# A Fourier and mixer kernel: a chunk's second product goes into the other PSUM bank, and the block sums move away from the GpSimd adds

## The chip, the cores and the metric

The kernel runs on one core of a Trainium2 chip. The metric is the device time of one execution, in microseconds. Three runs of the kernel before are given, and one more execution was taken with the hardware profiler; its trace is what the profile shows.

## What is computed

The input x has 8 batches of 3008 tokens with 256 features. The reference takes a Fourier transform along tokens and features and keeps the real part, and then applies a mixer block: two matrix products along the tokens and two along the features, each with a relu between and a residual added.

```python
X = np.fft.fft(x, axis=1)
X = np.fft.fft(X, axis=2)
x = X.real
xt = x.transpose(0, 2, 1)
h = np.maximum(xt @ w_tok1, 0.0) @ w_tok2
u = x + h.transpose(0, 2, 1)
h2 = np.maximum(u @ w_ch1, 0.0) @ w_ch2
return u + h2
```

The shapes are w_tok1 (3008, 256), w_tok2 (256, 3008), w_ch1 (256, 1536) and w_ch2 (1536, 256).

## The kernel before

**The stages of a batch.** `fold` (VectorE, called DVE here; lines 414 to 433) adds mirrored features of x into `eo`. `front` (lines 436 to 567) does the transform and the token mixing as a sequence of small pieces, each ended by a `yield`: pieces with pz (line 445), pieces with pw and w (lines 472 to 477), `tok1` (pt, line 488, and uv), `third` (pq and py, then ACT's qs, then two DVE adds into yt, lines 514 to 527), and the pieces that make `ut`, the transposed u of one chunk (pu, line 552, and a DVE add, line 560). The PSUM tiles of these pieces rotate through three buffers (`ps_f`).

**The chunks.** A batch has 6 chunks of 512 tokens. For each chunk `mm1` (lines 584 to 597) multiplies by w_ch1 in 12 tiles of 128 hidden features and ACT writes the relu into c1. `mm2` multiplies c1 by w_ch2. Most chunks do that in `mm2_sums` (line 620), which saves one block product in eight: c1 is seen as 2 by 2 blocks (token halves by hidden halves), w_ch2 as 2 by 2 blocks (hidden halves by feature halves), and 7 products of 12 matmuls of 128x128 each give the four output blocks. They need sums of blocks: those of the weights are made once (`weight_sums`), those of c1 are made per chunk on DVE by `block_sums` (lines 599 to 609). Its four entries are called sum 0 to sum 3 here. Sums 0, 1 and 3 go into the tile sb, sum 2 overwrites a block of c1. Each sum is made in two halves of three tiles: k from 0 to 2 while the chunk is still in `mm1`, k from 3 to 5 one chunk later. First chunk of batch 0, the last chunk of even batches and the last chunk of all are plain (line 579) and use no sums.

**The order of the work.** All orders are written out by hand; each engine runs its own queue in the order of the calls and waits on semaphores. The main loop (lines 772 to 817) has four steps s for each chunk c. A step calls `mm1` for three tiles, takes some pieces of `own` (the rest of this batch's front) and of `nxt` (the next batch's front), and calls step s of `mm2` for the chunk before; `plan` and `own_plan` say how many pieces stand in which of a batch's 24 steps. DVE's folds are taken from the eleventh step of a batch on in batches 1 to 5.

**The seven products.** The tiles px and py are two PSUM banks, each seen as two halves: pa is px, pb is py. Products are accumulated in pa[:,0] over the four steps, and ACT copies the intermediate states to the tile m (`keep`, line 638). The steps of `mm2_sums` are:

- step 0: a product into pa[:,0] and one into pa[:,1], keep(0), a DVE add of pa[:,1] and m into the output tile osb, and a GpSimd add of the residual rt (128x256)
- step 1: a product of sb[:,0] into pb[:,0], a product of sb[:,1] on top of pa[:,0], keep(1)
- step 2: a product on top of pa[:,0], keep(2), a DVE add from pb[:,0]
- step 3: a product on pa[:,0], a product with sb[:,2] on pb[:,0], two DVE adds (first from px, then from py), a GpSimd add of the residual (128x512), and the stores

The DVE and GpSimd adds go through `residual` (line 618). `edges` (line 611) copies one or two columns inside rt, which a transposing DMA has filled one chunk earlier (`turn_u`, line 571). GpSimd's queue also issues the loads of x (lines 128 and 118).

Of the kernel before, what the change touches and what calls it, by code (L numbers as in the profile page):

```python
# [40 lines left out]
def kernel(  # L41
# [9 lines left out]
    nc = tc.nc  # L51
# [17 lines left out]
    def ps_out(name):  # L69
        return psum.tile([P, 512], FP32, tag="o2", name=name, bufs=2)  # L70
# [4 lines left out]
    def dram(t, offset, ap):  # L75
        return bass.AP(tensor=t, offset=offset, ap=ap)
# [84 lines left out]
    for t in (tp, tq):  # L161
        for i in range(2):
            h = slice(64 * i, 64 * i + 64)
            nc.scalar.activation(
                out=t[h, :, 64 - 64 * i:128 - 64 * i],
                in_=pcol[h, :].unsqueeze(2).to_broadcast([64, NG, 64]),
                func=AFT.Copy, scale=0.0)
    nc.scalar.activation(out=w1m[64:128, NG - 1, :],
                         in_=pcol[64:128, :].to_broadcast([64, DTOK]),
# [43 lines left out]
    wc2 = const.tile([P, NCT, D], FP16, tag="wc2")  # L213
# [8 lines left out]
    HC = NCT // 2  # L222
    wst = const.tile([P, 4, HC, P], FP16, tag="wst")
# [8 lines left out]
    def swap_wc1(h):  # L232
        nc.sync.dma_start(out=wc1[1][:, h, :], in_=wc1[0][:, h, :])
        nc.sync.dma_start(out=wc1[1][0:1, h, :], in_=wc1[0][0:1, 1 - h, :])
# [172 lines left out]
    def align_w2(j):  # L407
        th, k = j // 4, slice(16 * (j % 4), 16 * (j % 4) + 16)
        copy(0, w2p[:, th, k, 0:NQ], w2v[:, th, k, :])
# [171 lines left out]
    def plain(b, c):  # L581
        return (b, c) == (0, 0) or c + 1 == NCH and (b % 2 == 0 or b + 1 == BB)
# [16 lines left out]
    def block_sums(c1, sb, k, which):  # L599
        hi = slice(HC + k.start, HC + k.stop)  # L600
        a11, a21 = c1[:, k, 0:D], c1[:, k, D:CW]
        a12, a22 = c1[:, hi, 0:D], c1[:, hi, D:CW]
        sums = ((sb[:, 0, k], a21, a22, AT.add),
                (sb[:, 1, k], sb[:, 0, k], a11, AT.subtract),
                (a21, a11, a21, AT.subtract),
                (sb[:, 2, k], a12, sb[:, 1, k], AT.subtract))
        for i in which:
            o, x, y, op = sums[i]
            nc.vector.tensor_tensor(out=o, in0=x, in1=y, op=op)  # L609

    def edges(rt, c):
        for o, i in ((D, 0), (0, P)) if c >= 3 else ((D, P),):
            nc.vector.tensor_copy(out=rt[:, :, o:o + 1], in_=rt[:, :, i:i + 1])

    lower, upper, turned_ = slice(0, P), slice(P, D), slice(D, P, -1)

    def residual(eng, o, x, y):
        eng.tensor_tensor(out=o, in0=x, in1=y, op=AT.add)  # L618

    def mm2_sums(b, c, c1, s, box):  # L620
        if s == 0:
            box["osb"] = work.tile([P, 4, D], FP32, tag="osb", name="osb", bufs=3)
            box["m"] = work.tile([P, 3, 2, P], FP32, tag="m", name="m")
            box["po"] = ps_out("px"), ps_out("py")
            edges(box["rt"], c)
        osb, rt, sb, m = (box[i] for i in ("osb", "rt", "sb", "m"))
        pa, pb = (p[:].rearrange("p (i t d) -> p i t d", i=2, t=2) for p in box["po"])

        def product(o, a, hi, w, first=False):
            for t in range(2):  # L630
                f = D * hi + P * t
                for k in range(HC):
                    nc.tensor.matmul(o[:, t], lhsT=a(k)[:, f:f + P], rhs=w(k),  # L633
                                     start=(first and t == 0 and k == 0),
                                     stop=(k == HC - 1), skip_group_check=True)

        def keep(i):
            nc.scalar.activation(out=m[:, i], in_=pa[:, 0], func=AFT.Copy)  # L638

        v, g = nc.vector, nc.gpsimd  # L640
        if s == 0:
            product(pa[:, 0], lambda k: c1[:, k], 0, lambda k: wc2[:, k, lower], True)
            product(pa[:, 1], lambda k: c1[:, HC + k], 0, lambda k: wc2[:, HC + k, lower])
            keep(0)
            residual(v, osb[:, 0:2, lower], pa[:, 1], m[:, 0])
            residual(g, osb[:, 0:2, lower], osb[:, 0:2, lower], rt[:, 0:2, lower])
        elif s == 1:
            product(pb[:, 0], lambda k: sb[:, 0, k], 0, lambda k: wst[:, 0, k], True)
            product(pa[:, 0], lambda k: sb[:, 1, k], 0, lambda k: wst[:, 1, k])
            keep(1)  # L650
        elif s == 2:
            product(pa[:, 0], lambda k: c1[:, k], 1, lambda k: wst[:, 2, k])
            keep(2)
            residual(v, osb[:, 2:4, upper], pb[:, 0], m[:, 2])
        else:
            product(pa[:, 0], lambda k: c1[:, HC + k], 1, lambda k: wst[:, 3, k])
            product(pb[:, 0], lambda k: sb[:, 2, k], 0, lambda k: wc2[:, HC + k, upper])
            residual(v, osb[:, 2:4, lower], pa[:, 0], rt[:, 2:4, lower])
            residual(v, osb[:, 0:2, upper], pb[:, 0], m[:, 1])
            residual(g, osb[:, :, upper], osb[:, :, upper], rt[:, :, turned_])  # L660
        if s == 3:
            for i in range(2):
                nk = 3 if c + 1 == NCH and i else 4
                nc.sync.dma_start(
                    out=dram(out_t, (b * S + 8 * c + i) * D,
                             [[NQ * D, 64], [2 * D, nk], [1, D]]),
                    in_=osb[64 * i:64 * i + 64, 0:nk, :])
            if c + 1 == NCH:
                nc.sync.dma_start(
                    out=dram(out_t, ((b - 1) * S + NQ - 1) * D, [[NQ * D, 64], [1, D]]),  # L670
                    in_=osb[64:P, 3, :])
# [45 lines left out]
    def pair(b, c1):  # L717

        if b % 2 == 0 and b + 1 < BB:
            state["ch"] = work.tile([P, NCT, 64], FP16, tag="ch", name="ch")  # L720
            nc.vector.tensor_copy(out=state["ch"][:], in_=c1[:, :, CW - 128:CW - 64])
        elif b % 2:
            nc.vector.tensor_copy(out=c1[:, :, CW - 64:CW], in_=state["ch"][:])


    def take(g, n):
        for _ in range(n):
            next(g, None)
# [41 lines left out]
    prev = None  # L770
    turned_u = {(0, 0): turn_u(0, 0)}
    for b in range(BB):
        nxt = front(b + 1) if b + 1 < BB else iter(())
        folds = fold(b + 2, [nc.vector] * 4) if b + 2 < BB else None
        for c in range(NCH):
            c1 = work.tile([P, NCT, CW], FP16, tag="c1", name="c1", bufs=2)
            box = {"rt": turned_u.pop((b, c))}
            if not plain(b, c):
                box["sb"] = work.tile([P, 3, HC, D], FP16, tag="sb", name="sb", bufs=2)
            if c + 1 == NCH and b % 2:  # L780
                pair(b, c1)
            for s in range(4):
                sub = 4 * c + s
                n = plan[b > 0][sub]
                mm1(b, c, c1, range(3 * s, 3 * s + 3))
                if s < 2 and prev is not None and not plain(*prev[0:2]):
                    block_sums(prev[2], pbox["sb"], slice(3, HC), (2 * s, 2 * s + 1))
                take(own, own_plan[b > 0][sub])
                take(nxt, n // 2)
                if prev is not None:  # L790
                    mm2(*prev, s, pbox)
                if s >= 2 and not plain(b, c):
                    block_sums(c1, box["sb"], slice(0, 3), (2 * s - 4, 2 * s - 3))
                if b == 0 and sub < 16 and sub % 2:
                    align_w2(sub // 2)
                take(nxt, n - n // 2)
                if s == 2 and c + 1 < NCH:
                    turned_u[b, c + 1] = turn_u(b, c + 1)
                if s == 3 and c + 1 == NCH and b + 1 < BB:
                    turned_u[b + 1, 0] = turn_u(b + 1, 0)  # L800
                if b == 0 and sub == 4:
                    weight_sums()
                if b == 0 and sub == 3:
                    for h in range(2):
                        swap_wc1(h)
                if b == 0 and 3 <= sub < 9:
                    take(early, 2)
                    if sub == 8:
                        x_tiles[2] = load_x(2)
                if folds is not None and sub >= fold_at[b > 0]:  # L810
                    take(folds, 1 + (b == 0))
                    if sub == fold_at[b > 0] + (5 if b == 0 else 11) and b + 3 < BB:
                        x_tiles[b + 3] = load_x(b + 3)
            if c + 1 == NCH and b % 2 == 0:
                pair(b, c1)
            prev, pbox = (b, c, c1), box
        own = nxt
# [32 lines left out]
```

## Time and profile before

| what | value |
|---|---|
| three runs, us | 618.13, 616.25, 618.18 |
| median, us | 618.13 |
| the profiled execution: its own time, us | 616.26 |
| the profiled execution: span of its trace, us | 614.2 |
| granted TensorE clock | 1.0 |
| block sums on DVE (line 609) | 336 instructions |
| edge copies on DVE (line 613) | 72, 0.18 us each on average |
| GpSimd adds of 128x512 (line 618) | 42, 1.44 us each on average |
| GpSimd adds of 128x256 (line 618) | 42, 0.76 us each on average |

The profile names a group of instructions by engine, line and tiles, out first: `osb<-px,m` is an add that reads the tiles px and m and writes osb. PE is TensorE, PEld its weight loads, ACT is ScalarE and POOL is GpSimd. A row of the timeline has the start in us, the duration in us, the engine, the line, the operation, the tiles and shapes, and the number of instructions merged in it; brackets give the idle time before it and what ended that. In the list of waits a row has the total in us, the number of times and the longest. A row for one line of the source has the least, the median and the greatest duration in ns.

### The profile page before, as it was taken

Reading aid. Unit: us, or ns where it says so; the run is one execution under the profiler, and the core shown is the slowest. Engines: PE = TensorE matmul, PEld = TensorE weight load, DVE = VectorE, ACT = ScalarE, POOL = GpSimd, SP = SyncE. Lnnn points to the kernel's source line nnn. Section 1 sums busy time; section 2 is a strip of 40 time slices with the busy share of each in tenths; the row PEclk is TensorE's granted clock in tenths of the full one; section 3 lists DMA queues with packets and bytes.
Section 4 is the critical chain, followed back from the end, with each engine's and each line's share of the span. In section 5 each row is a group of like instructions: output and inputs, shape, how many; then the busy total and the mean of one; then the engine's idle time right before and its main releaser. Section 6 shows DMA issues by size and latency. Waiting matters only on the chain.

```text
span 614.2 us, 15694 instructions
## 1 busy us (share of the span) xinstructions
PE 589.1 (96%) x6322; PEld 422.5 (69%) x6322; DVE 492.8 (80%) x1086; ACT 442.0 (72%) x996; POOL 139.3 (23%) x163
## 2 busy tenths in 40 slices
PE   2899999999999999999999999999999999999996
PEld 1766767667776767767676777766776767766675
DVE  8768879668998699768988789857899778867684
ACT  8866986677767777686766767777777777667772
POOL 8500413111142121302114221311121212101121
PEclk9999999999999999999999999999999999999999
DMA  8994842725347323672419234392222433232433
GB/s 137 210 192 93 183 67 56 162 57 84 53 89 141 85 52 68 118 120 52 97 44 174 53 83 74 61 183 61 53 62 58 91 53 75 65 69 60 88 62 94
DMA packets 86600, 56.52 MB, mean 92 GB/s; under 512 B 54864, under 2 KB 83472, under 8 KB 85776
## 3 DMA queue, kind: packets, MB, share of 16 engines
q1 hardware_dynamic: 78048, 37.84, 30.9%
q0 software_dynamic: 8256, 17.49, 16.5%
q8 instruction: 49, 0.80, 0.5%
q10 hardware_dynamic: 224, 0.20, 0.1%
q14 instruction: 23, 0.19, 0.1%
HBM read 34.98 MB, written 24.64 MB: 97 GB/s over the span
## 4 chain that ended last, share of the span: by engine, by line
PE 80%; DVE 8%; ACT 6%; issue 3%; POOL 1%; DMA 1%; DVEq 0%; POOLq 0%
PE pc L592 33%; PE px L633 20%; PE py L633 7%; PE pu L552 6%; PE po L690 4%; PE pt L488 3%; ACT c L595 3%; DVE sb L609 2%; DVE osb L618 2%; PE pz L445 1%; PE pw L472 1%; PE pw L473 1%; DVE ut L560 1%; PE py L519 1%; DVE yt L526 1%
## 5 line engine op out<-in xcount | busy, mean ns | idle before, releaser
L595 ACT ACTIVATE c<-pc 128x512 f16<-128x512 f32 (+1 forms) x572 | 295.8, 594 | 39.2 <-PE pc L592 19.8
L618 POOL TENSOR_TENSOR osb<-osb,rt 128x256 f32<-128x256 f32 x84 | 92.2, 1097 | 438.5 <-DVE osb L618 411.4
L592 PE MATMUL pc<-ut,wc1p 128*128 128x512 f16 x576 | 140.3, 379 | 0.0
L592 PE MATMUL pc<-ut,wc1m 128*128 128x512 f16 (+1 forms) x576 | 134.9, 370 | 0.0
L633 PEld LDWEIGHTS <-c 128*128 128x128 f16 x2016 | 121.3, 98 | 19.4 <-issue 0.3
L633 PEld LDWEIGHTS <-sb 128*128 128x128 f16 x1512 | 90.2, 98 | 14.1 <-issue 5.0
L638 ACT ACTIVATE m<-px 128x256 f32<-128x256 f32 x126 | 48.6, 386 | 69.9 <-PE px L633 45.2
L592 PEld LDWEIGHTS <-wc1p 128*128 128x128 f16 x576 | 52.2, 98 | 49.0 <-issue 2.3
L560 DVE TENSOR_TENSOR ut<-pu,yt 128x512 f16<-128x512 f32 (+1 forms) x96 | 64.1, 669 | 26.1 <-PE pu L552 26.1
L592 PEld LDWEIGHTS <-wc1m 128*128 128x128 f16 x576 | 53.0, 98 | 46.3
L609 DVE TENSOR_TENSOR sb<-c,sb 128x768 f16<-128x768 f16 x84 | 84.4, 1004 | 0.0
L633 PE MATMUL px<-wst,c 128*128 128x128 f16 x1008 | 70.0, 219 | 0.0
L633 PE MATMUL px<-wc,c 128*128 128x128 f16 x1008 | 63.1, 219 | 0.0
L618 DVE TENSOR_TENSOR osb<-py,m 128x256 f32<-128x256 f32 x84 | 35.4, 422 | 29.4 <-ACT m L638 23.2
L290 ACT ACTIVATE z<-pz 128x480 f16<-128x480 f32 (+1 forms) x60 | 40.1, 672 | 19.4 <-PE pz L445 12.4
L552 PE MATMUL pu<-w2p,uu 128*128 128x512 f16 (+1 forms) x168 | 50.0, 379 | 0.0
L609 DVE TENSOR_TENSOR c<-c 128x768 f16<-128x768 f16 x84 | 49.5, 590 | 0.0
L609 DVE TENSOR_TENSOR sb<-sb,c 128x768 f16<-128x768 f16 x84 | 46.9, 558 | 2.9
L609 DVE TENSOR_TENSOR sb<-c 128x768 f16<-128x768 f16 x84 | 45.9, 547 | 2.4 <-ACT c L595 2.4
L475 DVE SCALAR_TENSOR_TENSOR w<-alt,pw 128x131 f16<-128x131 f16 x96 | 33.0, 350 | 14.4 <-ACT w L290 14.3
L633 PE MATMUL px<-wst,sb 128*128 128x128 f16 x504 | 34.9, 219 | 3.2 <-DVE osb L618 2.6
L526 DVE TENSOR_TENSOR yt<-py,qs 128x512 f16<-128x512 f32 x48 | 30.8, 683 | 8.8 <-ACT qs L522 8.8
(163 smaller groups left out, 674.3 us busy)
## 6 DMA issues: line engine op xcount, KB each, us to landing
out_dram<-osb SPq DMA_DIRECT2D x83, 256.0 KB, 3.7
xp<-in_x_dram POOLq DMA_DIRECT2D x16, 272.0 KB
out_dram<-osb SPq DMA_DIRECT2D x11, 192.0 KB, 3.2
xp<-in_x_dram POOLq DMA_DIRECT2D x16, 127.5 KB
rt<-ut SPq DMA_TRANSPOSE x96, 3.4
w2s<-in_moe_w_tok_dram POOLq DMA_DIRECT2D x1, 1504.0 KB
w1p<-in_moe_w_tok_dram POOLq DMA_DIRECT2D x2, 384.0 KB
wc<-in_moe_w_ch_dram POOLq DMA_DIRECT2D x1, 768.0 KB
```

The lines of the kernel that those rows point to most:

```text
L290: nc.scalar.activation(out=out_, in_=in_, func=AFT.Copy)
L475: nc.vector.scalar_tensor_tensor(out=w[:, g, 0:131], in0=alt[:], scalar=pw[:, 131:132], in1=pw[:, 0:131], op0=AT.mult, op1=AT.add)
L526: nc.vector.tensor_tensor(out=yt[:, h, CW * c:CW * c + CW], in0=py[:], in1=qs[:], op=op)
L552: nc.tensor.matmul(pu[:, 0:n], lhsT=uu[:, th, int(minus), h, :], rhs=w2_cols(b, c)[:, th], start=(th == 0), stop=(th == 1))
L560: nc.vector.tensor_tensor(out=ut[:, h, 0:n].rearrange("p (a b) -> p a b", b=64), in0=pu[:, 0:n].rearrange("p (b a) -> p a b", b=64), in1=y ...
L592: nc.tensor.matmul(pc[:, 0:n], lhsT=wc[:, h, ct * P:(ct + 1) * P], rhs=ut[:, h, 0:n], start=(h == 0), stop=(h == 1))
L595: nc.scalar.activation(out=c1[:, ct, 0:n], in_=pc[:, 0:n], func=AFT.Relu)
L609: nc.vector.tensor_tensor(out=o, in0=x, in1=y, op=op)
L618: eng.tensor_tensor(out=o, in0=x, in1=y, op=AT.add)
L633: nc.tensor.matmul(o[:, t], lhsT=a(k)[:, f:f + P], rhs=w(k), start=(first and t == 0 and k == 0), stop=(k == HC - 1), skip_group_check=True)
L638: nc.scalar.activation(out=m[:, i], in_=pa[:, 0], func=AFT.Copy)
L690: nc.tensor.matmul(po[0:n, o:o + D], lhsT=c1[:, ct, ks * P:ks * P + n], rhs=wc2[:, ct, :], start=(ct == 0), stop=(ct == NCT - 1))
```

## The change

Four edits are made. The edge copies are issued by GpSimd. The second product of step 0 goes into pb[:,1] and opens that bank (its first matmul clears it), so that the add of step 0 reads py. In step 1 the product with sb[:,1] into pa[:,0] comes first and the one with sb[:,0] into pb[:,0] second, no longer as the first one of its bank. The calls of `block_sums` keep their contents and are placed anew in the step:

| step | before | after |
|---|---|---|
| 0 (sums 0 and 1, k from 3 to 5) | right after `mm1` | after the first pieces, ahead of `mm2` |
| 1 (sums 2 and 3, k from 3 to 5) | right after `mm1` | at the end, after the last pieces |
| 2 (sums 0 and 1, k from 0 to 2) | after `mm2` | after `mm2` |
| 3 (sums 2 and 3, k from 0 to 2) | after `mm2` | right after `mm1` |

```diff
     def edges(rt, c):
         for o, i in ((D, 0), (0, P)) if c >= 3 else ((D, P),):
-            nc.vector.tensor_copy(out=rt[:, :, o:o + 1], in_=rt[:, :, i:i + 1])
+            nc.gpsimd.tensor_copy(out=rt[:, :, o:o + 1], in_=rt[:, :, i:i + 1])
...
         if s == 0:
             product(pa[:, 0], lambda k: c1[:, k], 0, lambda k: wc2[:, k, lower], True)
-            product(pa[:, 1], lambda k: c1[:, HC + k], 0, lambda k: wc2[:, HC + k, lower])
+            product(pb[:, 1], lambda k: c1[:, HC + k], 0, lambda k: wc2[:, HC + k, lower], True)
             keep(0)
-            residual(v, osb[:, 0:2, lower], pa[:, 1], m[:, 0])
+            residual(v, osb[:, 0:2, lower], pb[:, 1], m[:, 0])
             residual(g, osb[:, 0:2, lower], osb[:, 0:2, lower], rt[:, 0:2, lower])
         elif s == 1:
-            product(pb[:, 0], lambda k: sb[:, 0, k], 0, lambda k: wst[:, 0, k], True)
             product(pa[:, 0], lambda k: sb[:, 1, k], 0, lambda k: wst[:, 1, k])
+            product(pb[:, 0], lambda k: sb[:, 0, k], 0, lambda k: wst[:, 0, k])
             keep(1)
...
                 mm1(b, c, c1, range(3 * s, 3 * s + 3))
-                if s < 2 and prev is not None and not plain(*prev[0:2]):
-                    block_sums(prev[2], pbox["sb"], slice(3, HC), (2 * s, 2 * s + 1))
+                def now():
+                    which = 2 * (s % 2), 2 * (s % 2) + 1
+                    if s >= 2 and not plain(b, c):
+                        block_sums(c1, box["sb"], slice(0, 3), which)
+                    elif s < 2 and prev is not None and not plain(*prev[0:2]):
+                        block_sums(prev[2], pbox["sb"], slice(3, HC), which)
+
+                if s == 3:
+                    now()
                 take(own, own_plan[b > 0][sub])
                 take(nxt, n // 2)
+                if s == 0:
+                    now()
                 if prev is not None:
                     mm2(*prev, s, pbox)
-                if s >= 2 and not plain(b, c):
-                    block_sums(c1, box["sb"], slice(0, 3), (2 * s - 4, 2 * s - 3))
+                if s == 2:
+                    now()
                 if b == 0 and sub < 16 and sub % 2:
                     align_w2(sub // 2)
                 take(nxt, n - n // 2)
+                if s == 1:
+                    now()
```

## The prediction

> **What bounds the kernel now.** I read the page's shares first, then the chain of work that ended last, the waits, and last the timeline step by step. A "step" is one s of a chunk c of batch b; sum 0 to sum 3 are the four entries of `block_sums`.
>
> The page, busy shares and the chain:
>
> ```profile
> PE 589.1 (96%) x6322; PEld 422.5 (69%) x6322; DVE 492.8 (80%) x1086; ACT 442.0 (72%) x996; POOL 139.3 (23%) x163
> ...
> PE 80%; DVE 8%; ACT 6%; issue 3%; POOL 1%; DMA 1%; DVEq 0%; POOLq 0%
> ```
>
> TensorE is the bound, and the change leaves each of its matmuls in place. So all that can be won is the time in which TensorE stands still. The waits name who holds it, and one row of line 609 shows why DVE is late:
>
> ```profile
> PE px L633 <- DVE osb L618: 2.6, 8, 0.8
> ...
> PE pz L445 <- DVE ut L560: 1.6, 3, 0.7
> ```
>
> ```profile
> L609 DVE TENSOR_TENSOR sb<-c,sb x84: 541/1025/2046, 59.4 to 599.6; 128x768 f16<-128x768 f16 x84
> ```
>
> The waits count only part of a gap, so I took the gaps from the timeline: the start of a product, plus twelve matmuls of 56 ns (0.67 us), against the start of the next. Batch 3, chunk 4, steps 0 and 1:
>
> ```profile
> 300.40 0.55 DVE L609 TENSOR_TENSOR c<-c 128x768 f16<-128x768 f16 x1
> 300.56 1.41 POOL L618 TENSOR_TENSOR osb<-osb,rt 128x512 f32<-128x512 f32 x1 [5.92 <-DVE osb L618]
> ...
> 300.87 1.52 DVE L609 TENSOR_TENSOR sb<-c,sb 128x768 f16<-128x768 f16 x1
> ...
> 304.13 0.83 PE L633 MATMUL py<-wst,sb 128*128 128x128 f16 x12
> 304.23 0.38 DVE L613 COPY rt<-rt 128x4 f16<-128x4 f16 x2
> 304.61 0.42 DVE L618 TENSOR_TENSOR osb<-px,m 128x256 f32<-128x256 f32 x1
> ...
> 305.09 0.83 PE L633 MATMUL px<-wst,sb 128*128 128x128 f16 x12
> ```
>
> The py product ends at 304.80, the px product starts at 305.09: 0.29 us lost, because it waits for the DVE add that reads px and ends at 305.03. That add stands behind sum 3, which took 1.52 instead of 0.55 while GpSimd added, and behind the two edge copies. The worst late sum 3, at the start of batch 4:
>
> ```profile
> 327.28 2.04 DVE L609 TENSOR_TENSOR sb<-c,sb 128x768 f16<-128x768 f16 x1
> ...
> 329.25 0.68 DVE L560 TENSOR_TENSOR ut<-pu,yt 128x512 f16<-128x512 f32 x1
> ...
> 329.98 0.37 PE L445 MATMUL pz<-t1n,eo 94*128 94x96 f16 x5 [0.72 <-DVE ut L560]
> ```
>
> Here pz wants the PSUM buffer that the late `ut` add still reads; 0.88 us are lost. The gaps of this kind from 80 us on, by place: c4 step 1 in batch 0, 1.18; in batches 1 to 5, 0.29 each, 1.45; c5 step 1, 0.37, 0.11, 0.72, 0.10, 0.37, none in batch 6, 0.36 in batch 7, 2.03; pz at c0 step 0 of batches 2, 4, 6, 0.88, 0.88, 0.35, 2.11; c0 step 1 of the same batches, 0.37 each, 1.11; w for `tok1` at c5 step 0 of batch 0, 1.28. Together 9.2 us, 1.5%: about the most that any reordering after the start can win.
>
> **What the Trainium skill says.** "SBUF — State Buffer", section "Who interferes with whom": a DVE instruction with two SBUF inputs contends with a GpSimd instruction that reads SBUF, and whichever comes second waits for the whole of the other. The trace agrees: sums and folds grow by up to 1.5 us beside the line 618 add of GpSimd, while the adds that read PSUM (lines 560, 618, 475) keep 0.68, 0.42 and 0.35 us. "PSUM — Partial Sum Buffer", section "PSUM bank collisions raise a hardware error": two engines may not touch one bank (in the same partitions) at once, so waits go by bank, not by address. That is why the product into pa[:,0] waits for an add that reads only pa[:,1].
>
> **The change, part by part.** Batch 3's times serve as the pattern. DVE starts follow each other by 0.58 (sum 0), 0.48 (sum 1), 0.46, 0.47, 0.34 (an add of line 618), 0.60 (`ut`), 0.26 (w); folds as in the rows, and a semaphore reaches TensorE 0.06 us after the end.
>
> *Second product of step 0 in py, and the exchange.* keep(0) now needs only the first product, and the first product of step 1 (px) only keep(0), which ACT finished at 303.35, 0.8 us before it is needed. The DVE add is needed 0.67 us later. The built program shows these waits: px on ACT, py on the DVE add. Cost: that first product reads sb[:,1], so sum 1 of k=3 to 5 is needed at its fourth matmul, 0.17 us after its start; before, only sum 0 was. Also py must now be free in step 0, 0.67 us after px: the add that frees it follows px's by 0.34, so this is free as long as px's is on time.
>
> *Edges to GpSimd.* 72 copies of 0.18 us leave DVE: 0.17 or 0.38 us ahead of the add of step 0. On GpSimd no row shows such a copy; its smallest ops at the start of the trace took 0.09 to 0.57 us. I take 0.2 each, bounds 0.1 and 0.6. GpSimd is 23% busy, and the readers of the edges (its own step 0 add, DVE's step 3 add, a plain chunk's add) come later; cost nothing. Cover gone: the out store moves by under 0.6 us, with three osb buffers behind it. Could they gain nothing? Yes, where DVE idled anyway.
>
> *Sums 2 and 3 of step 3 ahead of the adds of that step.* They no longer meet the GpSimd add: sum 3 falls from 1.52 to 0.55. But 0.93 us of sums now stand ahead of the adds that free px and py. Before c4 of batch 3: the fold started at 299.39, so sum 2 at 299.73, sum 3 at 300.19, the px add 300.66 to 301.08, the py add to 301.42. Products of step 0 start at 301.38 (px) and 302.05 (py): in time, by some 0.3 us. GpSimd's add starts at 301.5 and now meets the fold of line 431, which waits to 302.66 (1.16 us, the shortest such adds) and ends 303.07; w at 303.0; sum 0 at 303.26; sum 1 from 303.84 to 304.40; the add of step 0 ends at 304.8, wanted by py at 304.80 plus the stall. TensorE's px starts at 304.13 and needs sum 1 at 304.30; it sees it at 304.46: 0.16 lost, where it was 0.29. The same walk for c3 step 1, which had no gap, gives sum 1 visible at 293.96 against 293.86: 0.1 new, six batches, 0.6.
>
> *Sums 0 and 1 of step 0 behind the pieces of the front.* At c5 step 0 the piece is `third(0)`: two `yt` adds that wait for ACT's qs. Batch 4:
>
> ```profile
> 388.86 0.62 ACT L522 ACTIVATE qs<-pq 128x512 f32<-128x512 f32 x1
> ...
> 390.14 1.28 DVE L526 TENSOR_TENSOR yt<-py,qs 128x512 f16<-128x512 f32 x2
> ...
> 391.42 0.83 PE L633 MATMUL py<-wst,sb 128*128 128x128 f16 x12
> ```
>
> `yt` can start at 389.53 now, sum 0 at 390.75, sum 1 ends at 391.89, seen at 391.95; px needs it at 391.42+0.17=391.59: 0.36 lost in each of batches 1 to 6, 2.2 us in place of 1.67. Batch 7 has no such piece: its 0.36 goes. c0 step 1 of batches 2, 4, 6 (also behind `third`, one `pu` pair more for TensorE): sum 1 ends at 475.28 in batch 6, needed at 475.29: 0.1 each, 0.3 for 1.11.
>
> *Sum 3 clear of the add at the turn of a batch:* the `ut` add is 1 us earlier than pz: 2.11 goes. *Sums 2 and 3 of step 1 at its end:* a later GpSimd add is met less; sum 2 is seen at 307.1 against 307.3 (c4), 296.35 to 296.6 against 296.6 (c3): nothing, no more than 0.1 to spare. *Batch 0:* sum 1 at c4 seen at 87.5 against 86.8, 0.7 for 1.18; w at c5 has the same work ahead of it, 1.28 stays.
>
> Sum after: 0.7 + 5x0.16 + 2.2 + 0.3 + 0 + 0.6 + 1.28 = 5.9 us against 9.2. Gain 3.3 us. The profiled execution took 616.26 (span 614.2 and 2.1 around it), so 613.0. Two of the three runs stood at 618.1 and one at 616.25, the profile's level; from the median the same gain gives 614.9. I predict 614.0, between.
>
> **The rivals.** *All gaps go* (0.15): if qs and DVE come a little earlier than in my walk, only batch 0's 1.28 stays: 616.26-7.9=608.4, or 610.2 from the median. For it: each remaining stall is under 0.4. Against: at c5 the chain pq, qs, yt, sums cannot start sooner. *The wait changes its name* (0.22): sum 1 holds step 1 by 0.37 in c3, c4 and c5 of six batches, 6.7, plus 0.7 and 1.28: 8.7 for 9.2, 615.8, or 617.6. For it: three walks end within 0.2 of need. *Slower* (0.11): the sums ahead of step 3's adds hold px. It decides from 0.3 us of further delay on DVE at step 3 before c3 and c4 where folds run (12 places). At 0.6 us late, px waits 0.3 and sum 1 another 0.3: 7.2 us, less the 3.3: 620.2. Against it: no GpSimd add lies there. That the change does not do what it says is excluded by the waits of the built program.
>
> **How the numbers follow.** My case has 0.52, nearly all of it (0.49) faster by over 0.3%, which is about what a measurement of this kernel can tell from no change (1.9 us). With 0.15 that is 0.64 faster; 0.22 and 0.03 within, 0.25; 0.11 slower. The range, 609.8 to 618.4, covers my case at both levels, the renamed wait and the near part of the first rival; left out are the rest of that one and the slower case.
>
> **What would show it.** Right: sum 3 at about 0.55 us in most of its 84; line 431, 423 or 429 slower instead; "PE px <- DVE osb" gone; gaps of about 0.4 inside the first px product of c5 step 1, on sum 1; pz at the turn of a batch without wait. Wrong: px at step 0 waiting for the DVE add of the chunk before; sum 2 or 3 still near 1 us; edge copies on GpSimd of over 0.6 us.

## The result, and the profile after

The changed kernel took 612.88 us (median of four runs, 610.99 to 613.01) against 617.82 us before (616.25 to 618.18). The ratio is 0.9918, interval 0.9892 to 0.9944: 0.8% faster, some 5 us. The profiled execution took 613.01 us, its span is 611.2 us.

One thing is needed to read these numbers: every kernel here takes some 1.1 to 2.2 us more in some executions than in others, and in the traces that difference lies ahead of the first matmul of `mm1` (it starts at 38.4 to 38.5 us in nine, before among them, and at 40.3 to 40.5 us in five, after among them). So below I use, beside each ratio, two numbers of the trace. The *rest* is the span less the start of the first `mm1`. The *gaps* are the sum of all times over 0.06 us by which the start of a matmul in the rest comes later than its kind's usual distance from the matmul before; two short delays of 0.1 us, ahead of some pz and pt pieces and equal in all kernels, are left out.

| | rest, us | gaps, us | rest less gaps, us |
|---|---|---|---|
| before | 575.76 | 9.52 | 566.2 |
| after | 570.72 | 4.25 | 566.5 |

The rest fell by 5.0 us and the gaps by 5.3 us. What is left when the gaps are taken off moved by 0.2 us.

The page of the changed kernel, busy shares and the chain that ended last:

```profile
PE 589.9 (97%) x6322; PEld 423.5 (69%) x6322; DVE 455.7 (75%) x1014; ACT 447.2 (73%) x996; POOL 148.9 (24%) x235
...
PE 89%; DVE 5%; ACT 4%; issue 1%; DVEq 0%; POOL 0%; ACTq 0%; POOLq 0%
```

DVE lost 37 us of busy time (13 of them the edge copies), but that is not what counts: TensorE's share of the chain rose from 80 to 89%, because there are fewer places where the chain leaves it. The waits of TensorE and its weight loads on DVE have another name now:

```profile
PEld L633 <- DVE sb L609: 2.7, 7, 0.6
...
PE px L633 <- DVE sb L609: 1.5, 7, 0.4
```

The wait of px on the DVE add and that of pz on `ut` are gone from the list; seven waits on a block sum have come. Sum 3 and the edge copies, each by its line:

```profile
L609 DVE TENSOR_TENSOR sb<-c,sb x84: 542/551/1026, 59.6 to 596.0; 128x768 f16<-128x768 f16 x84
```

```profile
L613 POOL COPY rt<-rt x72: 192/203/1127, 46.5 to 603.3; 128x4 f16<-128x4 f16 x72
```

The median of sum 3 fell from 1025 to 551 ns. The place of the prediction's pattern, batch 3, chunk 4, steps 0 and 1, comes some 0.5 us earlier in this trace:

```profile
300.52 0.41 DVE L618 TENSOR_TENSOR osb<-py,m 128x256 f32<-128x256 f32 x1
...
301.07 1.48 POOL L618 TENSOR_TENSOR osb<-osb,rt 128x512 f32<-128x512 f32 x1 [6.72 <-DVE osb L618]
301.11 0.41 DVE L431 TENSOR_TENSOR eo<-xp 94x508 f16<-94x508 f16 x1
...
302.23 0.74 DVE L609 TENSOR_TENSOR sb<-c 128x768 f16<-128x768 f16 x1
...
302.50 1.13 POOL L613 COPY rt<-rt 128x4 f16<-128x4 f16 x2
303.00 0.56 DVE L609 TENSOR_TENSOR sb<-sb,c 128x768 f16<-128x768 f16 x1
303.48 0.42 DVE L618 TENSOR_TENSOR osb<-py,m 128x256 f32<-128x256 f32 x1
303.65 0.83 PE L633 MATMUL px<-wst,sb 128*128 128x128 f16 x12
...
304.32 0.83 PE L633 MATMUL py<-wst,sb 128*128 128x128 f16 x12
```

The two products start 0.67 us apart, so nothing is lost. The add ends at 303.90, 0.42 us ahead of the py product that waits for it. GpSimd's pair of copies takes 1.13 us here, beside DVE's sums, and nobody waits for it. The place where time is still lost is c5 step 1 of the same batch:

```profile
315.54 1.29 DVE L526 TENSOR_TENSOR yt<-py,qs 128x512 f16<-128x512 f32 x2 [0.93 <-ACT qs L522]
...
316.74 0.55 DVE L609 TENSOR_TENSOR sb<-c 128x768 f16<-128x768 f16 x1
...
317.22 0.33 PE L633 MATMUL px<-wst,sb 128*128 128x128 f16 x3
317.32 0.56 DVE L609 TENSOR_TENSOR sb<-sb,c 128x768 f16<-128x768 f16 x1
...
317.94 0.68 PE L633 MATMUL px<-wst,sb 128*128 128x128 f16 x9 [0.39 <-DVE sb L609]
```

The product stops after three of its twelve matmuls, at the first that reads the later half of sum 1. DVE had idled for 0.93 us before `yt`, waiting for ACT, while the sums stood behind `yt` in its queue.

### The profile page after: what moved, and what is told of

Its sections match the earlier page's. It is cut to its first block, busy times and chain, and to the rows that moved or that the text cites. A ratio compares the mean times of both kernels' runs of the same rounds, so it can differ in the third digit from the quotient of the medians.

```text
span 611.2 us, 15694 instructions
## 1 busy us (share of the span) xinstructions
PE 589.9 (97%) x6322; PEld 423.5 (69%) x6322; DVE 455.7 (75%) x1014; ACT 447.2 (73%) x996; POOL 148.9 (24%) x235
## 4 chain that ended last, share of the span: by engine, by line
PE 89%; DVE 5%; ACT 4%; issue 1%; DVEq 0%; POOL 0%; ACTq 0%; POOLq 0%
PE pc L592 38%; PE px L633 17%; PE py L633 13%; PE pu L552 7%; PE po L690 4%; PE pt L488 3%; PE pz L445 2%; ACT c L595 1%; DVE sb L609 1%; DVE yt L526 1%; PE pw L472 1%; PE pw L473 1%; PE filler L283 1%; PE py L519 1%; PE pq L519 1%
## 5 line engine op out<-in xcount | busy, mean ns | idle before, releaser
L618 POOL TENSOR_TENSOR osb<-osb,rt 128x256 f32<-128x256 f32 x84 | 79.3, 944 | 381.1 <-DVE osb L618 359.0
L618 DVE TENSOR_TENSOR osb<-py,m 128x256 f32<-128x256 f32 x126 | 52.9, 420 | 28.0 <-ACT m L638 24.2
L609 DVE TENSOR_TENSOR sb<-sb,c 128x768 f16<-128x768 f16 x84 | 50.3, 599 | 2.9
L609 DVE TENSOR_TENSOR sb<-c 128x768 f16<-128x768 f16 x84 | 47.6, 567 | 2.3 <-ACT c L595 2.3
L609 DVE TENSOR_TENSOR sb<-c,sb 128x768 f16<-128x768 f16 x84 | 47.2, 562 | 0.0
L609 DVE TENSOR_TENSOR c<-c 128x768 f16<-128x768 f16 x84 | 46.6, 554 | 0.0
L290 ACT ACTIVATE w<-pw 128x127 f16<-128x127 f32 x96 | 26.4, 282 | 22.3 <-PE pw L473 22.3
L633 PE MATMUL px<-wst,sb 128*128 128x128 f16 x504 | 36.6, 219 | 1.5 <-DVE sb L609 1.5
```

The lines of the kernel that those rows point to most:

```text
L290: nc.scalar.activation(out=out_, in_=in_, func=AFT.Copy)
L633: nc.tensor.matmul(o[:, t], lhsT=a(k)[:, f:f + P], rhs=w(k), start=(first and t == 0 and k == 0), stop=(k == HC - 1), skip_group_check=True)
```

## Experiments

The theory after the result: TensorE waits in step 1 because the DVE add of step 0 is late, and it is late by the sum of what stands ahead of it, a sum 3 held up by GpSimd and the edge copies. So the edges and the place of sum 3 win the time, the bank part (second product of step 0 in py, the exchange in step 1) wins nothing of its own, and the new places of sums 0 and 1 cost something. The rival: the shared bank was what held TensorE.

**The bank part alone.**

```diff
-            product(pa[:, 1], lambda k: c1[:, HC + k], 0, lambda k: wc2[:, HC + k, lower])
+            product(pb[:, 1], lambda k: c1[:, HC + k], 0, lambda k: wc2[:, HC + k, lower], True)
...
-            residual(v, osb[:, 0:2, lower], pa[:, 1], m[:, 0])
+            residual(v, osb[:, 0:2, lower], pb[:, 1], m[:, 0])
...
-            product(pb[:, 0], lambda k: sb[:, 0, k], 0, lambda k: wst[:, 0, k], True)
             product(pa[:, 0], lambda k: sb[:, 1, k], 0, lambda k: wst[:, 1, k])
+            product(pb[:, 0], lambda k: sb[:, 0, k], 0, lambda k: wst[:, 0, k])
```

> The kernel before with the bank part alone (second product of step 0 in py, step 1's products exchanged); sums and edges as before. Theory 1 (DVE's queue makes the add of step 0 late, the bank only moves the deadline inside the same pair of products): the add still stands behind the pieces and the two edge copies and is still wanted 0.67 us into step 1, so the gaps at c4 step 1 (0.29), c5 step 1 and c0 step 1 stay, and so does pz (0.88, 0.88, 0.35): within 0.5 us of the kernel before. Theory 2 (the shared bank was what held TensorE): the 5.8 us of gaps in step 1 go, about 612.

Measured: ratio 0.9993 (0.9983 to 1.0002), rest 575.4, gaps 9.09. The timeline of batch 3, c4 step 1:

```profile
303.86 0.83 PE L633 MATMUL px<-wst,sb 128*128 128x128 f16 x12
303.96 0.38 DVE L613 COPY rt<-rt 128x4 f16<-128x4 f16 x2
304.37 0.42 DVE L618 TENSOR_TENSOR osb<-py,m 128x256 f32<-128x256 f32 x1
...
304.85 0.83 PE L633 MATMUL py<-wst,sb 128*128 128x128 f16 x12 [0.15 <-DVE osb L618]
```

The wait has only changed its name, from px to py: 304.85 less 303.86 less 0.67 is 0.32 us, where it was 0.29. The rival falls for this part by itself.

**The edges alone.**

```diff
-            nc.vector.tensor_copy(out=rt[:, :, o:o + 1], in_=rt[:, :, i:i + 1])
+            nc.gpsimd.tensor_copy(out=rt[:, :, o:o + 1], in_=rt[:, :, i:i + 1])
```

> The kernel before with the edge copies on GpSimd alone. Theory 1: the add of step 0 comes 0.38 us earlier where c is 3 or more, so the gaps of 0.29 at c4 and of 0.37 at c5 and c0 of step 1 close, 0.72 falls to 0.34; pz at the turn of a batch keeps 2.1 us. Gain 4 to 4.6 us, most of what the whole change gave. Theory 2: edges are a small part of DVE's queue; gain under 1 us.

Measured: ratio 0.9911 (0.9886 to 0.9937), rest 571.0, gaps 4.73. All gaps of step 1 outside batch 0 are gone, that of 0.72 too, of which I had expected 0.34 to stay; pz keeps 2.12 and batch 0 has 2.5. The gain in the gaps is 4.8 us, nearly that of the whole change. In the timeline of the same place only a w piece stands between the sums and the add, which is 0.15 us ahead of its reader:

```profile
302.50 0.83 PE L633 MATMUL py<-wst,sb 128*128 128x128 f16 x12
302.60 0.42 DVE L618 TENSOR_TENSOR osb<-px,m 128x256 f32<-128x256 f32 x1
...
303.17 0.83 PE L633 MATMUL px<-wst,sb 128*128 128x128 f16 x12
```

**The sums alone** (the placement hunk of the change, with the edges and the banks of before).

```diff
+                if s == 3:
+                    now()
...
+                if s == 0:
+                    now()
                 if prev is not None:
                     mm2(*prev, s, pbox)
...
+                if s == 1:
+                    now()
```

> The kernel before with the new places of the block sums alone. Theory 1: pz at the turn of a batch loses its gap (2.1 us won), but the sums of step 0 now stand behind the pieces and ahead of the edge copies and the add, so that the add is 0.3 to 0.6 us late in step 1 of c3, c4 and c5 of six batches and 0.3 in c0 of three: gaps of 10 to 11 us against 9.2, so 0 to 2 us slower. Theory 2 (the collisions with GpSimd's add are the whole cost): gain of 3 us or more.

Measured: ratio 0.9981 (0.9972 to 0.9991), rest 574.8, gaps 8.44. The pz gaps are gone (2.1 us), c5 step 1 has risen from 2.02 to 3.59, c2 step 2 has 0.54 new, c4 1.17 for 1.45, c0 0.63 for 1.11. The size was off, and so was the sign: I had 0.3 to 0.6 each for c3, which has nothing, and for c4, which has 0.23. That much of the theory stands: c5 pays back most of what is won elsewhere.

**Sums and edges, without the bank part.** Both edits above together.

> The changed kernel without its bank part: sums and edges as in it, the second product of step 0 in px and the products of step 1 in the old order. Theory 1: the first product of step 1 needs only sum 0, the second the add, which ends 0.34 to 0.42 us after sum 1; so the gap of 0.32 at c5 step 1 becomes 0.2, that of c4 goes, pz has none. As fast as the changed kernel or up to 1.5 us faster. Theory 2: without the second bank the gaps in step 1 come back, 4 to 6 us slower than the changed kernel.

Measured: ratio 0.9905 (0.9881 to 0.993), rest 570.2, gaps 3.82 against 4.25 in the changed kernel. c5 step 1 has 0.91 for 2.15, as its first product needs only sum 0; c2 step 2 has 0.54 for none. Batch 0 has some 0.6 us more. On balance the bank part is not what earns the change's gain.

**Edges, and of the sums only those of step 3.**

```diff
+                if s == 0 or s == 1 or s == 3:
+                    now()
```

> The kernel before with the edge copies on GpSimd and, of the sums' new places, only that of step 3 (sums 2 and 3 right after the first matmuls); steps 0 and 1 and the banks as before. Theory 1 (edges ahead of the add cost the gaps of step 1, sum 3 beside the GpSimd add costs pz, and the later places of sums 0 and 1 and the bank part cost rather than win): no gap at c5 step 1, none at pz, none at c2 step 2; only batch 0 keeps 2.0 to 2.6 us. Some 2 us faster than the changed kernel. Theory 2 (sums 0 and 1 must leave the GpSimd add too, or they block DVE for 1 us and the add of step 0 is late again): gaps of 0.3 in step 1 of c4 and c5, no faster than the changed kernel.

Measured: ratio 0.9892 (0.9868 to 0.9917), rest 569.1, gaps 2.70, all in batch 0 but for 0.06. The rest and the gaps are 1.6 us less than in the changed kernel, although the bank part and two of the three moves of the sums are left out. The intervals of the two ratios overlap; the lowest times, 609.32 and 610.99, differ by 1.7 us.

**The changed kernel with the sums of step 0 put back.**

```diff
-                if s == 3:
+                if s == 0 or s == 3:
                     now()
...
-                if s == 0:
-                    now()
```

> The changed kernel with sums 0 and 1 of step 0 put back right after the first matmuls. Theory 1: its gaps of 0.32 to 0.55 inside the first product of c5 step 1 (2.15 us in six batches) and those of 0.07 at c4 go, since sum 1 no longer stands behind yt; 2 us faster than the changed kernel. Theory 2: sums 0 and 1 meet the GpSimd add of 128x512, one of them takes 1.5 us, and what follows on DVE is late: no gain, or slower.

Measured: ratio 0.9888 (0.9864 to 0.9911), rest 568.9, gaps 2.57. c5 step 1 has no gap left. Batch 3 shows why, at c5 step 0:

```profile
314.25 0.55 DVE L609 TENSOR_TENSOR sb<-c 128x768 f16<-128x768 f16 x1
314.61 0.62 ACT L522 ACTIVATE qs<-pq 128x512 f32<-128x512 f32 x1
...
314.83 0.56 DVE L609 TENSOR_TENSOR sb<-sb,c 128x768 f16<-128x768 f16 x1
...
315.31 1.28 DVE L526 TENSOR_TENSOR yt<-py,qs 128x512 f16<-128x512 f32 x2
```

The sums stand in the time in which DVE waited for ACT in the changed kernel, and `yt` starts 0.08 us after qs has ended. Elsewhere sums 0 and 1 do meet the GpSimd add, as the second theory said: 27 of the 168 take over 1.1 us. At c4 step 0 of the same batch:

```profile
301.17 1.52 DVE L609 TENSOR_TENSOR sb<-c 128x768 f16<-128x768 f16 x1
...
303.46 0.42 DVE L618 TENSOR_TENSOR osb<-py,m 128x256 f32<-128x256 f32 x1
...
304.04 0.83 PE L633 MATMUL py<-wst,sb 128*128 128x128 f16 x12
```

Sum 0 takes 1.52 us and it costs nothing, because the add, with no copies ahead of it, still ends 0.16 us before its reader starts.

**Each edge copy twice on DVE.**

```diff
             nc.vector.tensor_copy(out=rt[:, :, o:o + 1], in_=rt[:, :, i:i + 1])
+            nc.vector.tensor_copy(out=rt[:, :, o:o + 1], in_=rt[:, :, i:i + 1])
```

> The kernel before with every edge copy issued twice on DVE (the result is the same). Theory 1: the add of step 0 comes 0.34 us later where c is 3 or more, and each of the 15 to 16 gaps of step 1 at c4, c5 and c0 grows by about that: 4.5 to 5.5 us slower than the kernel before. Theory 2 (edges fill idle time of DVE): within 1 us of it.

Measured: ratio 1.0105 (1.0079 to 1.013), rest 582.4, gaps 16.30, so 6.6 us slower. The gaps at c4 went from 0.29 to 0.71, those at c0 from 0.37 to 0.79: 0.42 for each added pair, somewhat more than the 0.34 I had put down. At these places the copies are on the path with their whole length.

**Bank part and sums, without the edges.** The changed kernel with the copies on DVE.

> The changed kernel with the edge copies back on DVE (bank part and sums as in it). Theory 1: the add of step 0 is late again by the two copies, the wait only moves from the px product to the py product: gaps of 7.5 to 8.5 us against 4.25 in the changed kernel, that is 3 to 4 us slower than it and 1 to 2 us faster than the kernel before. Theory 2 (the later deadline of the bank part hides the copies): within 1 us of the changed kernel.

Measured: ratio 0.9966 (0.9953 to 0.9978), rest 574.0, gaps 7.47. As expected: c5 step 1 now loses 2.16 at px (on sum 1) and 1.43 at py (on the add), c4 1.19 at py. The bank part does not hide the copies; against the sums alone (gaps 8.44) it is worth 1.0 us of gaps.

**Only the sums of step 3 moved**, on the kernel before.

> The kernel before with sums 2 and 3 of step 3 right after the first matmuls, and nothing else changed (edges on DVE, old banks, sums of steps 0 and 1 in their old places). Theory 1: pz at the turn of a batch has no gap (2.11 us won), since the ut add no longer stands behind a sum 3 of 2 us; the gaps of step 1 stay within 0.1 us each, because the edge copies still stand ahead of the add. Gain of 2 to 2.5 us. Theory 2 (sum 3's collision also causes the gaps of step 1): gain of 5 us or more.

Measured: ratio 0.9933 (0.9906 to 0.996), rest 571.9, gaps 5.65. The pz gaps are gone, c4 (1.38) and c0 (1.20) stay; but c5 fell from 2.02 to 0.15, which I had not expected, so the gain in the gaps is 3.9 us and lies between the theories. The timeline at the start of batch 4 shows both halves:

```profile
324.78 0.55 DVE L609 TENSOR_TENSOR sb<-c,sb 128x768 f16<-128x768 f16 x1
324.95 1.19 POOL L118 DMA_INDIRECT xm<-in_x_dram,ix  x1 [0.30 <-issue]
...
325.91 0.68 DVE L560 TENSOR_TENSOR ut<-pu,yt 128x512 f16<-128x512 f32 x1
...
326.16 1.17 POOL L618 TENSOR_TENSOR osb<-osb,rt 128x512 f32<-128x512 f32 x1
...
326.51 1.25 DVE L609 TENSOR_TENSOR sb<-c 128x768 f16<-128x768 f16 x1
327.27 0.38 PE L445 MATMUL pz<-t1n,eo 94*128 94x96 f16 x5
...
329.47 0.38 DVE L613 COPY rt<-rt 128x4 f16<-128x4 f16 x2
329.85 0.42 DVE L618 TENSOR_TENSOR osb<-px,m 128x256 f32<-128x256 f32 x1
...
330.32 0.83 PE L633 MATMUL px<-wst,sb 128*128 128x128 f16 x12 [0.27 <-DVE osb L618]
```

Sum 0 takes over the wait for the GpSimd add (1.25 us), but behind `ut`, so pz is on time; the DVE add behind the copies still is not.

**Without the GpSimd add of step 3**, on the kernel before.

```diff
-            residual(g, osb[:, :, upper], osb[:, :, upper], rt[:, :, turned_])
```

> The kernel before without the GpSimd add of 128x512 in step 3: the residual of the upper half of the features is left out of the chunks with sums. Theory 1: sum 3 takes 0.55 us everywhere, DVE is 1 us earlier at step 0, and the gaps of steps 0 and 1 outside batch 0 close (6.7 us), edges or not: 6 to 7.5 us faster than the kernel before. Theory 2 (sum 3 is long for another reason, for instance its own operands): it stays above 1 us, and the time stays within 1 us.

The result lacks the residual of the upper half of the features in the chunks with sums. Measured: ratio 0.9858 (0.9836 to 0.988), rest 568.2, gaps 1.92, of which 0.15 outside batch 0. Sum 3:

```profile
L609 DVE TENSOR_TENSOR sb<-c,sb x84: 542/550/1029, 61.5 to 593.5; 128x768 f16<-128x768 f16 x84
```

The median is 550 ns, so the long sum 3 was that add's doing. I had written 0.55 us everywhere, which is not so: 15 of the 84, all in step 1, still take 1.02 to 1.03 us, beside the smaller GpSimd add of step 0. With the edges still on DVE all gaps of step 1 but two are closed.

**Edges, step 3 and step 1, without the bank part.** The kernel with sum 0 early less its bank part.

> The changed kernel without its bank part and with the sums of step 0 right after the first matmuls; it differs from the earlier kernel with sum 0 early only in the bank part. Theory 1: the bank part is worth at most a few tenths: gaps within 0.7 us of that kernel's 2.57, of which 0.54 because keep(1), and so w and sum 2 at c2 step 2, come later without it. Theory 2 (the bank part is needed once the rest is right): 2 us or more slower than that kernel.

Measured: ratio 0.9889 (0.9867 to 0.9911), rest 570.1, gaps 3.75. Against 2.57 the bank part is worth 1.2 us here, more than I allowed: 0.54 at c2 step 2, where without it keep(1) comes after both products, and some 0.6 in batch 0 and around it, most of that at c4 step 1 (0.68 for 0.25).

**The folds of batch 0 spread**, on the kernel with sum 0 early, to close the gaps that were left.

```diff
-    fold_at = [15, 10]
+    fold_at = [14, 10]
...
-                    take(folds, 1 + (b == 0))
-                    if sub == fold_at[b > 0] + (5 if b == 0 else 11) and b + 3 < BB:
+                    take(folds, 1 + (b == 0 and sub < 16))
+                    if sub == fold_at[b > 0] + (9 if b == 0 else 11) and b + 3 < BB:
```

> The changed kernel with the sums of step 0 right after the first matmuls and, in batch 0, the 12 folds for batch 2 spread: two in each of steps 14 and 15, one in each of steps 16 to 23, instead of two in each of steps 15 to 20. Theory 1: what is left are the gaps of batch 0 (about 2.3 us), where DVE has two folds in a step; with one, the late w at c5 step 0 (1.0) and the gaps of c4 fall by half or more: 1 to 1.5 us faster. Against it: the folds of steps 21 to 23 stand beside third and the ut adds and can open new gaps there.

Measured: 608.51 us, ratio 0.9871 (0.9842 to 0.9899), the lowest time of all that compute everything; rest 568.3, gaps 1.93. The late w fell from 1.0 to 0.41, but 0.62 is new at c4 step 0 and 0.54 stands at c4 step 1, so it gained 0.6 us and not 1 to 1.5. Its interval overlaps those of the other early-sum kernels; the order among them rests on rest and gaps.

In all fourteen kernels the rest less the gaps lies between 566.1 and 566.5 us. So the kernels differ in the gaps alone; no matmul ran at another pace.

## Why the prediction was right, point by point

**The bound and its ceiling.** That only TensorE's gaps could be won, some 9.2 us of them, held: in every kernel the rest changed by what its gaps changed, within 0.3 us.

**The bank part.** The add is wanted later and sum 1 is needed at the fourth matmul, as forecast; the trace of after shows both. What the prediction did not say is that this part alone wins next to nothing: 0.4 us of gaps alone, -0.4 in the changed kernel, 1.0 beside the sums without the edges, 1.2 where sum 0 is early. Its worth depends on what is late beside it.

**The edges.** 0.2 us each on GpSimd was right for the median (203 ns); 27 of the 72 took over 0.3 us and the longest 1.13, beyond my bound of 0.6. One add waited for them, 1.68 us in the last chunk, and no matmul was late for it. What I had missed is their gain, which I counted only inside the walks. They are the largest single part: 4.8 us of gaps alone, and without them the changed kernel has 7.47 instead of 4.25.

**Sums 2 and 3 of step 3.** Sum 3 at 0.55 us and px in time were right. So was the new meeting, in seven of the ten places where a fold stands behind the GpSimd add (c3 and c4 of batches 1 to 5): there the fold takes 1.40 to 1.41 us. At c4 of batch 2:

```profile
230.08 1.16 POOL L618 TENSOR_TENSOR osb<-osb,rt 128x512 f32<-128x512 f32 x1 [6.78 <-DVE osb L618]
230.12 1.40 DVE L431 TENSOR_TENSOR eo<-xp 94x508 f16<-94x508 f16 x1
```

The step that was mis-sized is "which waits to 302.66 (1.16 us, the shortest such adds) and ends 303.07". It puts the fold's full 0.41 us behind the add's end; measured, the fold ends 0.28 us behind it (231.52 against 231.24), 0.13 less, and that moves the sums. So the gaps at c4 are 0.07 in four batches for my 0.16 in five. At c3, where I saw 0.1 coming, sum 1 is seen 0.11 us early (batch 2). Together that is 0.28 us for 1.4.

In the other three places the fold did not wait at all. One is c4 of batch 3, shown above: the fold starts at 301.11, again 0.04 us behind the add's recorded start, and takes its plain 0.41, while the add takes 1.48 us instead of 1.16. What stood behind waited instead, sum 0, and only for 0.2 us (0.74 for 0.55). "SBUF — State Buffer", section "Who interferes with whom", says that the order of issue decides who waits. The recorded starts are 0.04 us apart in both cases, so this trace can't confirm it; I had given the order to GpSimd everywhere.

**Sums 0 and 1 behind the front's pieces.** 0.36 for each of six batches was predicted; 0.32 in five and 0.55 in one, where ACT's qs ended 0.23 us later against the product, were measured: 2.15 us for 2.2. At c0 step 1 I had 0.1 each, and nothing was lost.

**The rest.** pz at the turn of a batch: 2.11 gone, as said. Batch 7: gone. Batch 0 at c4: 0.7 predicted, 0.66 measured in two pieces. Its late w: kept at 1.28, measured 0.98 in two pieces.

**The sum.** 5.9 us of gaps were predicted, 4.25 measured, and before has 9.52 by the same count, not 9.2; so 5.3 were won instead of 3.3. The terms too large are c3 (0.6), c4 (0.5), c0 (0.3) and the late w (0.3). The 2.1 us around the span, carried over, became 1.8. The predicted 614.0 us lies 1.1 above the measured 612.88, and that nearness is partly luck: 614.0 was set between two sums, 613.0 from the profiled execution of before (616.26) and 614.9 from its median, and against 610.99, the lowest time of after, the first of these is 2.0 us too high.

**The rivals.** "The wait changes its name" is what happened at c5 and, with 0.07 us, at c4, not at c3. "All gaps go" did not happen in the changed kernel, since c5 keeps 2.15 us; with sum 0 early they nearly do, outside batch 0. "Slower" did not occur: px was in time at step 0 everywhere.

**Two causes, one gap.** The gains of the parts do not add up, and I had not seen why before the runs. Edges alone win 4.8 us, step 3's sums alone 3.9, both together 6.8. At c5 the runs show that taking away one of the two is enough: without the copies no gap is left, with sum 3 moved 0.15 us, so the second can win next to nothing there. At c4 and c0 moving the sums of step 3 does not help, since sum 0 then meets the GpSimd add in their place (1.5 us at c4, 1.1 to 1.25 at c0); without that add the gaps close with the copies still there.

## What to carry to other kernels

When one engine is busy nearly all the time, add up its gaps by place from the start times, and walk each gap back along the queue of the engine that ends it: what stands ahead of an awaited instruction that is already late has its full price, a copy of 0.2 us as well as a collision of 1 us. Change the parts of a combined edit one by one, since two of them may close the same gap and a third may open a new one: here the edge copies and one of the three moves of the sums left less of the gaps than all four edits did. Work that is ready belongs ahead of an instruction that waits for another engine: behind `yt` the sums of step 0 cost 2.15 us of gaps, ahead of it none. A collision that comes with such a place costs nothing as long as the next awaited instruction is still in time, by 0.16 us here.

## What the runs showed of the hardware that I had not expected

**TensorE ran at half its rate for longer in some executions.** In the trace of before, 24 filler matmuls of 128 columns at 21.43 us take 1.34 us up to the next product, 56 ns each; in that of after, at 22.20 us, 2.57 us, 107 ns each. The first trace:

```profile
21.43 1.50 PE L283 MATMUL filler<-anti,ident 128*128 128x128 f16 x24
22.77 0.59 PE L445 MATMUL pz<-t1n,eo 94*128 94x96 f16 x10
```

and the second:

```profile
22.20 2.76 PE L283 MATMUL filler<-anti,ident 128*128 128x128 f16 x24
24.77 0.63 PE L445 MATMUL pz<-t1n,eo 94*128 94x96 f16 x9
```

In both a pz piece starts at 20.57 us; the next one comes 2.20 us later in the first trace and 4.20 in the second, with the same matmuls between, although the granted clock reads 1.0 there in both. TensorE is at about half its rate for some 4 us longer in the second, which loses the 2 us by which `mm1` starts later. It goes with no edit, since the times of the kernel before differ by as much among themselves. What decides it stays open; no run was made for it.

**A recorded start on GpSimd does not tell who waits.** In the changed kernel a fold starts 0.04 us behind the recorded start of the same kind of GpSimd add in ten places. In seven the fold takes 1.40 to 1.41 us and the add 1.16 to 1.17; in three the fold takes its plain 0.41 to 0.42 and the add 1.48. With sum 0 early it is one place against nine. What decides it stays open.

**A gather on GpSimd did not hold up a sum.** In the kernel with only step 3's sums moved, sum 3 kept 0.55 us with a gather starting 0.17 us into it. That is one place, and no run was made for it.
